# Splitting the loads of suf, pre and ekb into 2, 2 and 4 DMAs in a recurrent-attention and two-layer MoE kernel

## The chip, the cores and the metric

The kernel runs on one core of a Trainium2 chip. The metric is the device time of one execution in microseconds (us), median of the runs. Five engines work side by side, each through its own list of instructions in a fixed order: PE (matmuls; PEld loads its weights), DVE, ACT and POOL (elementwise work), and SP, which here issues every DMA. The core has 16 DMA engines that move the data.

## The reference

Four batches, 8 heads, 768 steps, head size 40. A state of 40 x 40 per head is decayed, corrected by one row and one column, and read out:

```python
for t in range(S):
    y[:, :, t] = einsum('bhd,bhde->bhe', rt, state)
    Sa = einsum('bhde,bhe->bhd', state, at)
    state = state * wt[:, :, None, :] - einsum('bhd,bhe->bhde', Sa, bt) \
            + einsum('bhd,bhe->bhde', vt, kt)
```

The result, as 3072 tokens of 320 numbers, goes through two layers `g(x @ w_in) @ w_out` with 2048 hidden units; g is a piecewise square in the first layer and `s * relu(h)**2 + b` in the second. The weights come as 64-bit numbers and are turned into 32-bit ones on the chip.

## The kernel before

**Attention** goes in 24 chunks of 32 steps; two chunks make a unit, so there are 12 units, u = 0 to 11. For each unit three arrays are loaded into 104 partitions: `suf` (429 KB, rows of 4224 bytes) and `pre` (416 KB, rows of 4096 bytes), from which DVE makes products of the decays by scans (L375, L384), and `ekb` (832 KB, rows of 8192 bytes), keys and b, which are multiplied by `suf` (L445, POOL from the second unit on). PE forms `ap` from `ekb` and `xa` (L466); its copy `am` is stored to `ascr` (L479) and loaded again as `la` (L555) and `aa` (L585). DVE inverts a triangular matrix in `ln` from `la` in 15 steps of two instructions (L566, L569), the "inverse"; it is stored to `lscr` (L571) and loaded as `lt` (L589), which `pl` (L598), `pq` and `up` on PE need. From there a chain runs chunk by chunk: `xp`, `up`, `sp` (state), `tp`, `gg`, `py` (the chunk's output) and `ptx`.

`suf`, `pre` and `ekb` have one buffer each. The buffer of `pre` is also that of `am`: the next unit's `pre` can be loaded only when both stores to `ascr` have landed. The next `ekb` can be loaded when the unit's `ap` matmuls and the copies to `tk` and `tb` are through.

**The MoE** takes blocks of 256 tokens (two chunks) in layer 1 (L954 into `h`, L985 into `acc`) and 512 tokens in layer 2 (L964, L1003). Layer 1 runs between the attention's steps; layer 2 follows it. Before the first block has its input, PE runs matmuls on weights whose result is not used (L1034, the "spare matmuls"); their number is fixed when the program is written out.

**The order** of the instructions on every engine is written out by a planner (`Order`) that runs when the program is built. Every piece of work is a thread that yields operations with an assumed duration; the planner gives each engine the ready thread that is due first. For a DMA it assumes 475 ns of SP for each issue and bytes / 360 ns of transfer, and at most eight DMAs on their way at a time. `dma(nbytes, fn, count, flag)` yields such an operation; `count` is the number of DMAs that `fn` issues. So a changed count changes the planned times, and with them the order on all five engines. On the chip the DMAs use eight completion semaphores in turn: each waits until the DMA eight before it has landed.

Of the kernel before, what the change touches and what calls it, by code (L numbers as in the profile page):

```python
# [221 lines left out]
def dma(nbytes, fn, count=1, flag=None, each=475):  # L222

    op = Op("SP", each * count, fn, 980, flag, nbytes / 360)
    op.count = count
    return op
# [22 lines left out]
def fast_path(ctx, tc, inside, ws_em, wp_em, a_em, kb_em, v_em, r_em, v_tok, eye, mask_a, mask_g, eye_kb,  # L249
              w1_in, w1_out, w2_in, w2_out, sb, out):  # L250
    nc = tc.nc
# [136 lines left out]
    tks, tes, lt_t = {}, {}, {}  # L388
    both = lambda n, c: ((n + "0", c), (n + "1", c))

    def loads_e():
        for u in range(NU):
            yield due("loads", u)
            yield Acq("es")
            suf = emp.tile([104, 2 * NP, C + 1], F32, tag="es", name="suf")
            yield dma(104 * 4224, lambda: nc.sync.dma_start(out=suf.rearrange("p a t -> p (a t)"), in_=ws_em[u]), 1, ("lw", u + 1))
            sufs[u] = suf

            def pre():
                yield Acq("ew")  # L400
                pre = emp.tile([104, 2 * NP, C], F32, tag="ew", name="pre")
                pres[u] = pre
                yield dma(104 * 4096, lambda: nc.sync.dma_start(out=pre.rearrange("p a t -> p (a t)"), in_=wp_em[u]), 1, ("lp", u + 1))

            def keys():
                yield Acq("ekb")
                ekb = emp.tile([104, 2, 2 * NP, C], F32, tag="ekb", name="ekb")
                ekbs[u] = ekb
                yield dma(104 * 8200, lambda: nc.sync.dma_start(out=ekb.rearrange("p x a t -> p (x a t)"), in_=kb_em[u]), 1, ("lk", u + 1))

            if u == 0:
                yield from pre()
            yield from keys()
            if u:
                yield from pre()
# [651 lines left out]
    for g in (loads_e(), loads_a(), setup(), clear(), prep_a(), inverse(), loads_x(), mend(), keys(), decays(), loads_t(), loads_v(), loads_r(),  # L1067
              chain_a(), chain_b(), warm(), ychunk(), xchunk(), moe(), loads_w(0), loads_w(1),
              *(convert(l, part, odd) for l in range(2) for part in range(2) for odd in range(2))):
        od.add(g, 0, Start.ready)  # L1070
# [94 lines left out]
def rwkv_moe_kernel(tc, out, **ins):  # L1165
    nc = tc.nc
    with tc.tile_pool(name="flag", bufs=1, space=DRAM) as fp:
        flag = fp.tile([1, 1], I32, name="flag")
        nat = {n: ins.pop(n) for n in "rkvwab"}
        with tc.manual_schedule():  # L1170
            fast_path(tc, flag, out=out, **ins)
        inside = nc.values_load(flag[0:1, 0:1], min_val=0, max_val=128)
        with tc.If(inside < 128):
            general_path(tc, nat, ins["eye"], ins["w1_in"], ins["w1_out"], ins["w2_in"], ins["w2_out"], ins["sb"], out)
# [66 lines left out]
```

## Time and profile before

| | |
|---|---|
| median of 3 runs | 1236.17 us (1234.88 to 1250.49) |
| the profiled execution: its time, its span | 1242.7 us, 1240.9 us |
| PE, PEld busy | 1125.5 us (91%), 1025.2 us (83%) |
| DVE, ACT, POOL busy | 736.5 us (59%), 757.4 us (61%), 360.9 us (29%) |
| moved by DMA | 107.36 MB |

The span is the time from the first to the last instruction in the trace. Busy shares are over the whole span; a start stage (to about 160 us), a stage with attention and layer 1 together (to about 700 us), the rest of layer 1 (to about 870 us) and layer 2 differ from one another. In a timeline, the bracket behind a row gives how long the engine stood idle before it and what ended that wait. In a chain of waits, a DMA's piece runs from its issue to its landing.

### The profile page before, as it was taken

To read this page: it belongs to the slowest core of one execution; us is meant where nothing else is said; L and a number is where in the kernel's file an instruction comes from. 1 tells how busy PE (TensorE), PEld (TensorE's weight loads), DVE (VectorE), ACT (ScalarE), POOL (GpSimd) and SP (SyncE) were. 2 spreads that over 40 slices of the span, in tenths; PEclk is the share of its full clock that TensorE was granted. 3 is DMA by queue.
4 is the path that set the end of the run, shared out by engine and by line. 5 is a ranking of instruction groups with operands and counts; after the bars stand their busy time and mean duration, and the time that the engine had idled before them with its cause. 6 is when DMAs were issued, how large, how long until landed. Compare 5 with 4: busy or idle time off the path is not lost.

```text
span 1240.9 us, 47386 instructions
## 1 busy us (share of the span) xinstructions
PE 1125.5 (91%) x20654; PEld 1025.2 (83%) x20654; DVE 736.5 (59%) x1629; ACT 757.4 (61%) x1537; POOL 360.9 (29%) x333
## 2 busy tenths in 40 slices
PE   3897899889898989989899999999999999999995
PEld 3796788778787778878788889999888889888895
DVE  4775877666568676777647343277974344444432
ACT  2433767557476565765666677688765555555553
POOL 5555563414143331323421112366540000000000
PEclk9898699899899988989999999999999999999998
DMA  7875525464555546474432210156201010101000
GB/s 195 239 199 138 125 58 124 91 140 99 110 108 109 124 95 126 81 149 104 96 79 61 44 43 14 34 172 205 69 1 48 1 47 4 45 10 26 16 7 24
DMA packets 188415, 107.36 MB, mean 87 GB/s; under 512 B 149126, under 2 KB 167686, under 8 KB 186950
## 3 DMA queue, kind: packets, MB, share of 16 engines
q1 hardware_dynamic: 188198, 104.24, 35.4%
q8 instruction: 164, 2.69, 0.9%
q14 instruction: 53, 0.43, 0.1%
HBM read 78.25 MB, written 19.66 MB: 79 GB/s over the span
## 4 chain that ended last, share of the span: by engine, by line
PE 72%; DVE 8%; ACT 5%; issue 5%; DMA 5%; SPq 1%; POOL 1%; DVEq 0%; ACTq 0%; POOLq 0%
PE h L954 14%; PE h L964 12%; PE acc L985 12%; PE acc L1003 12%; PE h L1034 6%; PE gg L819 2%; PE sp L747 2%; PE tq L768 2%; PE ap L466 2%; PE py L840 1%; PE xp L709 1%; PE up L724 1%; DMA lt<-lscr 1%; PE tp L802 1%; PE ptx L873 1%
## 5 line engine op out<-in xcount | busy, mean ns | idle before, releaser
L934 POOL TENSOR_TENSOR gl<-g,gh 128x512 fp32r<-128x512 f32 x96 | 125.4, 1306 | 433.9 <-ACT gh L932 380.0
L954 PE MATMUL h<-xh,w 128*128 128x256 f32 x1152 | 228.1, 301 | 5.7 <-DVE g L922 2.9
L954 PEld LDWEIGHTS h<-xh,w 128*128 128x128 f32 x1152 | 182.2, 198 | 12.4 <-issue 3.9
L985 PE MATMUL acc<-w,gh 128*128 128x320 f32 x768 | 190.6, 335 | 0.0
L1003 PE MATMUL acc<-w,gh 128*128 128x320 f32 x768 | 173.1, 312 | 2.6 <-ACT o L1016 2.1
L932 ACT CAST gh<-g 128x512 fp32r<-128x512 f32 x192 | 118.9, 619 | 61.1 <-DVE g L922 37.1
L1003 PEld LDWEIGHTS acc<-w,gh 128*128 128x128 f32 x768 | 132.2, 189 | 11.6 <-ACT o L1016 3.9
L934 DVE TENSOR_TENSOR gl<-g,gh 128x512 fp32r<-128x512 f32 x96 | 68.1, 709 | 117.7 <-ACT gh L932 117.5
L985 PEld LDWEIGHTS acc<-w,gh 128*128 128x128 f32 x768 | 130.9, 198 | 5.0 <-issue 0.2
L985 PE MATMUL acc<-w,gl 128*128 128x320 f32 x384 | 123.0, 320 | 0.0
L1003 PE MATMUL acc<-w,gl 128*128 128x320 f32 x384 | 118.7, 309 | 0.0
L928 ACT ACTIVATE g<-g,sbt 128x512 f32<-128x512 f32 x96 | 78.3, 816 | 64.8 <-DVE g L926 64.7
L954 PE MATMUL h<-xl,w 128*128 128x256 f32 x384 | 111.5, 290 | 0.4 <-issue 0.4
L922 DVE SCALAR_TENSOR_TENSOR g<-h,g 128x512 f32<-128x512 f32 x96 | 66.1, 688 | 75.1 <-ACT h L921 46.4
L919 ACT ACTIVATE g<-h,sbt 128x512 f32<-128x512 f32 x96 | 65.9, 687 | 64.8 <-PE h L954 61.7
L926 DVE SCALAR_TENSOR_TENSOR g<-h,g 128x512 f32<-128x512 f32 x96 | 66.3, 691 | 60.7 <-ACT g L925 60.6
L925 ACT ACTIVATE g<-h 128x512 f32<-128x512 f32 x96 | 57.2, 596 | 72.1 <-PE h L964 72.1
L1034 PE MATMUL h<-w 128*128 128x256 f32 x668 | 91.5, 299 | 0.0
L1034 PEld LDWEIGHTS h<-w 128*128 128x128 f32 x668 | 87.1, 204 | 1.4 <-issue 0.3
L238 POOL TENSOR_TENSOR t<-t,w 128x384 int32<-128x384 int32 x64 | 67.6, 1060 | 68.3 <-DVE t L236 41.0
L759 DVE TENSOR_TENSOR xr<-sp,pc 40x320 f32<-40x320 f32 x92 | 44.8, 487 | 58.4 <-PE sp L747 56.9
L964 PE MATMUL h<-xx,w 128*128 128x512 f32 x288 | 76.8, 402 | 2.1 <-DVE w L330 2.1
(107 smaller groups left out, 2277.7 us busy)
## 6 DMA issues: line engine op xcount, KB each, us to landing
w<-in_w_in SPq DMA_DIRECT2D x32, 384.0 KB
w<-in_w_out SPq DMA_DIRECT2D x32, 320.0 KB
ekb<-in_kb_em SPq DMA_DIRECT2D x12, 832.0 KB
tk<-ekb SPq DMA_DIRECT2D x48, 128.0 KB
suf<-in_ws_em SPq DMA_DIRECT2D x12, 429.0 KB
pre<-in_wp_em SPq DMA_DIRECT2D x12, 416.0 KB
xa<-in_a_em SPq DMA_DIRECT2D x48, 80.0 KB
xr<-in_v_tok SPq DMA_DIRECT2D x48, 80.0 KB
```

The lines of the kernel that those rows point to most:

```text
L238: (pool, n, lambda: nc.gpsimd.tensor_tensor(out=t, in0=t, in1=lo, op=ALU.add)),
L919: yield act(512, lambda: nc.scalar.activation(out=g, in_=h, func=AF.Relu, bias=sbt[:, 2:3]), more=93)
L922: yield dve(512, lambda: nc.vector.scalar_tensor_tensor(out=g, in0=h, scalar=1.0, in1=g, op0=ALU.subtract, op1=ALU.add))
L926: yield dve(512, lambda: nc.vector.scalar_tensor_tensor(out=g, in0=h, scalar=0.0, in1=g, op0=ALU.max, op1=ALU.mult))
L928: yield act(512, lambda: nc.scalar.activation(out=g, in_=g, func=AF.Identity, scale=sbt[:, 0:1], bias=sbt[:, 1:2]), more=230)
L932: yield act(512, lambda: nc.scalar.copy(out=gh, in_=g))
L934: yield mk(512, lambda: eng.tensor_tensor(out=gl, in0=g, in1=gh.bitcast(F32), op=ALU.subtract))
L954: yield pe(8 * 118, lambda: [nc.tensor.matmul(h[:, i, :], lhsT=a, rhs=b, start=m == 0, stop=m == 7) for m, (a, b) in enumerate(mm)])
L964: yield pe(4 * 224, lambda: [nc.tensor.matmul(h, lhsT=a, rhs=b, start=4 * i + m == 0, stop=4 * i + m == 7) for m, (a, b) in enumerate(mm[4 ...
L985: yield pe(6 * 147, lambda: [nc.tensor.matmul(acc[0, n][u], lhsT=a, rhs=b, start=p == 0 and m == 0, stop=p == NFF // 2 - 1 and m == 5) for ...
L1003: yield pe(3 * 147, lambda: [nc.tensor.matmul(acc[1, n][u], lhsT=a, rhs=b, start=f == 0 and m == 0, stop=f == NFF - 1 and m == 2) for m, ( ...
L1034: yield pe(2 * 109, lambda: [nc.tensor.matmul(h[:, i, :], lhsT=wh[:, 0:128], rhs=wh[:, 0:256], start=True, stop=True) for i in range(2)], ...
```

## The change

The three loads go through a new helper that cuts the rows of an array into k equal parts and issues one DMA for each. `suf` and `pre` become two DMAs of 104 rows of 2112 and 2048 bytes, `ekb` four of 104 rows of 2048 bytes. The planner is told the new counts. What is loaded, and where to, stays.

```diff
+    def pieces(out, src, k):
+        n = src.shape[-1] // k
+        for i in range(k):
+            nc.sync.dma_start(out=out[:, i * n:i * n + n], in_=src[:, i * n:i * n + n])
+
...
-            yield dma(104 * 4224, lambda: nc.sync.dma_start(out=suf.rearrange("p a t -> p (a t)"), in_=ws_em[u]), 1, ("lw", u + 1))
+            yield dma(104 * 4224, lambda: pieces(suf.rearrange("p a t -> p (a t)"), ws_em[u], 2), 2, ("lw", u + 1))
...
-                yield dma(104 * 4096, lambda: nc.sync.dma_start(out=pre.rearrange("p a t -> p (a t)"), in_=wp_em[u]), 1, ("lp", u + 1))
+                yield dma(104 * 4096, lambda: pieces(pre.rearrange("p a t -> p (a t)"), wp_em[u], 2), 2, ("lp", u + 1))
...
-                yield dma(104 * 8200, lambda: nc.sync.dma_start(out=ekb.rearrange("p x a t -> p (x a t)"), in_=kb_em[u]), 1, ("lk", u + 1))
+                yield dma(104 * 8200, lambda: pieces(ekb.rearrange("p x a t -> p (x a t)"), kb_em[u], 4), 4, ("lk", u + 1))
```

In all, 827 DMAs become 887, and 668 spare matmuls become 650; every other count of instructions stays. Lines behind the helper lie five further down in the changed kernel (L445 is L450 there). Three places show how the order moves.

**DVE at the start.** Before, the first rows after the scans of `suf` (t<-w is the first weight, turned to 32 bits):

```order
L384 SCALAR_TENSOR_TENSOR pre<-pre,start_p 104x256
L235 TENSOR_SCALAR t<-w 128x384
L383 RECIPROCAL start_p<-suf 104x8
L236 SCALAR_TENSOR_TENSOR t<-w,t 128x384
L384 SCALAR_TENSOR_TENSOR pre<-pre,start_p 104x256
L235 TENSOR_SCALAR t<-w 128x320
L445 TENSOR_TENSOR ekb<-ekb,suf 104x1024 x2
```

The same place in the changed kernel:

```order
L383 RECIPROCAL start_p<-suf 104x8
L384 SCALAR_TENSOR_TENSOR pre<-pre,start_p 104x256
L450 TENSOR_TENSOR ekb<-ekb,suf 104x1024 x2
L459 TENSOR_TENSOR xa_112<-xa_112,pre 40x512 x2
L459 TENSOR_TENSOR xa_113<-xa_113,pre 40x512 x2
L235 TENSOR_SCALAR t<-w 128x384
L236 SCALAR_TENSOR_TENSOR t<-w,t 128x384
```

The work on the weights, which stood among that on `pre`, `ekb` and `xa`, now stands behind all of it. On SP the first two weight loads move from behind `mska` to behind all eight `xa` loads.

**PE up to the first `pl`.** Before:

```order
L1034 MATMUL h<-w 128x256 x84
L466 MATMUL ap<-ekb,xa_113 32x64 x32
L1034 MATMUL h<-w 128x256 x30
L709 MATMUL xp<-xr_102,xa_112 32x40 x32
L1034 MATMUL h<-w 128x256 x212
L466 MATMUL ap<-ekb,xa_114 32x64 x32
L1034 MATMUL h<-w 128x256 x14
L466 MATMUL ap<-ekb,xa_115 32x64 x32
L1034 MATMUL h<-w 128x256 x198
L598 MATMUL pl<-lt,aa 32x16 x32
```

And now:

```order
L1039 MATMUL h<-w 128x256 x70
L471 MATMUL ap<-ekb,xa_113 32x64 x32
L1039 MATMUL h<-w 128x256 x48
L714 MATMUL xp<-xr_102,xa_112 32x40 x32
L1039 MATMUL h<-w 128x256 x216
L471 MATMUL ap<-ekb,xa_114 32x64 x32
L1039 MATMUL h<-w 128x256 x10
L471 MATMUL ap<-ekb,xa_115 32x64 x32
L1039 MATMUL h<-w 128x256 x182
L603 MATMUL pl<-lt,aa 32x16 x32
```

The spare matmuls ahead of the first `pl` go from 538 to 526, and those behind it from 130 to 124.

**SP around the `ekb` load of u = 4.** Before:

```order
L571 DMA lscr2_166<-ln_105 64x512 x2
L409 DMA ekb_3594<-in_kb_em 104x2048
L479 DMA ascr3_155<-am_3350 128x8x32
L694 DMA ggr_108<-in_r_em 40x512 x2
L589 DMA lt_3550<-lscr2_166 128x8x32
L403 DMA pre_3678<-in_wp_em 104x1024
L555 DMA la_3599<-ascr3_155 64x16x16 x2
```

And now:

```order
L394 DMA ekb_3561<-in_kb_em 104x512 x4
L699 DMA ggr_108<-in_r_em 40x512 x2
L484 DMA ascr3_155<-am_3328 128x8x32
L576 DMA lscr2_166<-ln_105 64x512 x2
L594 DMA lt_3659<-lscr2_166 128x8x32
L560 DMA la_3658<-ascr3_155 64x16x16 x2
L394 DMA pre_3706<-in_wp_em 104x512 x2
```

The store to `lscr` now stands behind `ekb`, and `la` stands ahead of `pre`. Such swaps go both ways over the units: a store to `lscr` stands close behind `ekb` in three units before (u = 3, 7, 11) and in three now (u = 3, 4, 6).

## Rows read from the trace of the kernel before

**Rows 1.** The page: share of the span by engine.

```profile
span 1240.9 us, 47386 instructions
PE 1125.5 (91%) x20654; PEld 1025.2 (83%) x20654; DVE 736.5 (59%) x1629; ACT 757.4 (61%) x1537; POOL 360.9 (29%) x333
```

**Rows 2.** Busy us by stage; PEclk is the granted clock's share, DMA the engines'.

```profile
core 0: us, PE busy (x) PEld busy (x) DVE busy (x) ACT busy (x) POOL busy (x), PEclk, DMA share, GB/s
0.00:160.00 160.00, 123.39 (x2257) 116.51 (x2258) 113.20 (x239) 68.16 (x161) 86.98 (x89) 0.87 0.68 177
160.00:700.00 540.00, 481.77 (x13925) 432.18 (x13924) 361.40 (x937) 342.11 (x753) 177.15 (x145) 0.92 0.48 102
700.00:870.00 170.00, 167.82 (x2529) 160.57 (x2529) 85.07 (x161) 132.35 (x261) 67.67 (x63) 1.00 0.29 91
870.00:1241.00 371.00, 352.53 (x1949) 315.92 (x1947) 176.85 (x294) 214.77 (x365) 29.07 (x36) 0.98 0.09 24
```

**Rows 3.** Chain that ended last: shares of the span by engine.

```profile
PE 72%; DVE 8%; ACT 5%; issue 5%; DMA 5%; SPq 1%; POOL 1%; DVEq 0%; ACTq 0%; POOLq 0%
```

**Rows 4.** The chain in order of time: start us, us, what.

```profile
214.70 6.70 DMA lt<-lscr
...
266.60 4.28 DMA lt<-lscr
...
324.34 2.38 DMA lscr<-ln
...
378.16 5.36 DMA ascr<-am
383.66 4.56 DMA pre<-in_wp_em
...
587.79 6.88 DMA lscr<-ln
594.72 2.42 DMA lt<-lscr
```

**Rows 5.** Timeline of SP around three `ekb` loads: start us, us, instruction.

```profile
78.14 0.40 SPq L409 DMA_DIRECT2D ekb<-in_kb_em  x1
78.65 0.38 SPq L479 DMA_DIRECT2D ascr<-am  x1
...
89.66 0.33 SPq L403 DMA_DIRECT2D pre<-in_wp_em  x1
...
212.50 0.50 SPq L409 DMA_DIRECT2D ekb<-in_kb_em  x1
...
586.28 0.31 SPq L409 DMA_DIRECT2D ekb<-in_kb_em  x1
```

**Rows 6.** Columns as Rows 2, stretches with one kind of load each.

```profile
5.10:7.20 2.10, 0.00 (x0) 0.00 (x0) 2.00 (x4) 1.28 (x1) 2.10 (x3) 1.00 1.05 250
7.20:11.80 4.60, 0.00 (x0) 0.00 (x0) 3.09 (x7) 0.25 (x1) 3.46 (x4) 1.00 0.85 191
12.50:15.50 3.00, 0.00 (x0) 0.00 (x0) 2.16 (x6) 2.29 (x5) 1.06 (x1) 1.00 0.70 251
329.70:335.10 5.40, 4.33 (x200) 3.84 (x201) 4.96 (x10) 2.93 (x8) 0.61 (x1) 1.00 0.84 178
337.50:340.20 2.70, 2.08 (x14) 1.99 (x14) 0.01 (x1) 1.62 (x4) 0.00 (x0) 0.59 0.93 191
```

**Rows 7.** What SP waited for in 0 to 13 us: total, times, longest.

```profile
SPq L424 <- DMA ekb<-in_kb_em: 4.3, 1, 4.3
SPq L424 <- DMA pre<-in_wp_em: 1.7, 1, 1.7
SPq L424 <- DMA suf<-in_ws_em: 0.9, 1, 0.9
```

**Rows 8.** DVE and PE at the end of the first inverse (timeline).

```profile
94.03 0.69 DVE L384 TENSOR_TENSOR_SCAN pre<-pre,start_p 104x256 f32<-104x256 f32 x1 [4.22 <-DMA w<-in_w_in]
...
105.58 1.05 PE L598 MATMUL pl<-lt,aa 32*32 32x16 f32 x64 [5.36 <-issue]
```

**Rows 9.** The page: the spare matmuls, busy and mean ns of one.

```profile
L1034 PE MATMUL h<-w 128*128 128x256 f32 x668 | 91.5, 299 | 0.0
```

**Rows 10.** DVE in the first 20 us (timeline).

```profile
13.34 0.36 DVE L235 TENSOR_SCALAR t<-w 128x384 int32<-128x384 int32 x1 [2.88 <-ACT w L233]
13.74 0.56 DVE L236 SCALAR_TENSOR_TENSOR t<-w,t 128x384 int32<-128x384 int32 x1
```

**Rows 11.** SP's issue of `pre` and `ekb`: ns min/median/max.

```profile
L403 SPq DMA_DIRECT2D pre<-in_wp_em x12: 307/316/2103, 1.3 to 595.5; - x12
L409 SPq DMA_DIRECT2D ekb<-in_kb_em x12: 308/367/662, 1.6 to 586.3; - x12
```

## The prediction

> **What bounds the kernel now.** I read the page first for the busy shares, then the busy time by stage, then the chain of waits, and last the timelines of SP and DVE around the three loads that change. The page [rows 1] says that PE is the engine to watch: 91% busy, no other over 61%. The stages [rows 2] say where the other 9% lie. From 700 to 870 us PE works 167.82 of 170 us, and layer 2 is nearly as full up to its last stores; none of the three loads is issued there, and nothing can be gained. In the start stage PE is idle for 160 - 123.39 = 37 us, and from 160 to 700 us for 540 - 481.77 = 58 us. Those 95 us are all that a change in loads can work on, and only the part that ends in a DMA: 5% of the chain, 62 us over the whole span, is DMA [rows 3].
>
> The pieces of the chain [rows 4] tell which DMAs. They are hardly the three loads: once it is `pre` (4.56 us), otherwise `lt`, `lscr` and `ascr`, small transfers of 128 KB or less that take 2.38 and 2.42 us when they go alone, and 6.70 and 6.88 us in two other places. SP's timeline [rows 5] has the reason: the 6.70 us at 214.70 start 2.2 us after an `ekb` load was issued (212.50), the 6.88 us at 587.79 1.5 us after another (586.28). A small transfer issued behind the 832 KB of `ekb` lands when those are through. So `ekb` costs by what waits behind it, about 4.4 us each time (6.88 - 2.38, 6.70 - 2.42).
>
> **The `ekb` load in four.** The bytes stay. What may change is their rate, and the trace has no load of 104 rows of 2 KB, so it is bounded. From 7.20 to 11.80 us nearly all that moves is `ekb`, rows of 8 KB: 191 GB/s with the DMA engines 85% busy, so they are at work and slow [rows 6]. From 12.50 to 15.50 us, mostly `xa` loads with rows of 2 KB and weight rows of 3 KB, 251 GB/s come out of only 70%. One end: no gain. Other end: `ekb`'s 13 of 16 engines (104 rows in equal shares) at the second stretch's rate per busy engine, 251 / 0.70 x 13/16 = 291 GB/s, or 852 kB in 2.9 us instead of 4.5 us at 191 GB/s: 1.5 us less. The nearest row is `pre`, half the row length on the same 104 partitions: in the middle of the run it moved at 191 GB/s against 178 for `ekb` [rows 6], 7% better for a row half as long, which would be 0.3 us. The rows halve twice, and the early stretch of `pre` (250 GB/s, partly `ekb`'s own bytes) speaks for more. I take 0.7 us per load, estimated between these rows, ends 0 and 1.5 us. The rate pays where something on the chain stands behind `ekb`: four places in rows 4 (214.70, 266.60, 378.16 with 383.66, 587.79), and one at the start. There `ekb` is issued at 78.14, the store to `ascr` behind it at 78.65, `pre`, which needs that store, only at 89.66 [rows 5]; DVE stands 4.22 us in the middle of the inverse until 94.03 for its scan of `pre`, 4.4 us after that issue, although the wait is labelled with a weight [rows 8]. Five places by 0.7 us: **-3.5 us**; ends 0 and 11 loads by 1.5, -16.5 us.
>
> Three more issues at 0.37 us (median, [rows 11]) put the next DMA on SP 1.1 us later. What hides that is `ekb` itself: what stands behind waits over 4 us for its bytes, not for its issue. Taken at 0; if that cover went, five places by 1.1, +5.5 us.
>
> On batching, the Trainium skill (DMA: Bandwidth & Descriptors, Rules for kernel authors) says the opposite of this change: for most bandwidth, 128 partitions and at least 1 MiB per DMA, and many small transfers should be coalesced into one. By that alone 832 KB in one DMA would be better than in four of 208 KB, and the sum would turn positive. The trace does not agree in the stretch just named: DMAs of at most 384 KB moved 251 GB/s there, against 191 for one of 832 KB.
>
> **`suf` and `pre` in two.** One more issue each, 0.32 us for `pre` [rows 11], against a somewhat better rate. `suf` is loaded long before its scans; only `pre` is on the chain. I put the two at 0, ends 0.3 us either way at five places, 1.5 us.
>
> **The new order at the start.** 18 spare matmuls fewer, at 91.5 / 668 = 0.137 us [rows 9], are 2.5 us. Twelve of them stand ahead of the first `pl`, where PE idles 5.36 us anyway [rows 8]: they shorten nothing. The six behind it: **-0.8 us**. The `pl` wait itself ends with the first inverse on DVE. Up to there DVE has one first and two second steps of a weight fewer (0.36 + 2 x 0.56 us, [rows 10]) and one scan of `pre` fewer (0.69, [rows 8]): 2.2 us. And DVE no longer idles 2.88 us for the first weight between two scans of the first `pre` [rows 10], since the weights now stand behind. On the other side the first two weight loads go behind all `xa` loads. DMAs go at most eight at a time: the ninth to eleventh waited for `suf`, `pre` and `ekb`, 0.9, 1.7 and 4.3 us [rows 7]. The eight pieces now fill that allowance alone, so the first weights land some 2 to 3 us later (by the length of the `xa` stretch, 12.50 to 15.50), and the spare matmuls with them. I take **-2 us** of the 5.36; ends -5.36 and +3 us.
>
> **The sum.** -3.5 - 0.8 - 2 = -6.3 us against the profiled execution of 1242.7 us (span 1240.9): 1236.4 us. That execution lies 6.5 us above the median 1236.17 us of the runs; against the median the forecast is **1230 us**. The ends: -16.5 - 1.5 - 0.8 - 5.4 gives 1212, +5.5 + 1.5 + 3 gives 1246.
>
> **Rivals.** *The row length is not what slows `ekb`.* The slow rate may belong to 104 partitions on 13 engines; `pre` and `ekb` are within 7% in mid-run (191, 178). Then only the start's -2.8 us are left: 1233 us. Chance 0.20. The Trainium skill (SBUF — State Buffer, Door 1: The DMA port swizzle) has DMA bandwidth depend on how many of SBUF's ports the partitions reach; by it pieces on the same partitions would gain nothing. The rates of rows 6 do not exclude that.
>
> *The full gain*: 291 GB/s, and all 11 later loads count, with the start's best: about 1212 us. For it: engines busy and slow in every `ekb` stretch. Against it: in seven units nothing of `ekb` is on the chain. Chance 0.10.
>
> *The new order is the worse one.* In u = 4 the store to `lscr` now stands behind `ekb`: 6.88 instead of 2.38 us, +4.5. There `lt` stood behind `ekb` before (6.70 instead of 2.42 us), which gives most back; in u = 6 `lt` stood ahead, and the 4.5 us are lost. Two or three such places: 1230 + 14 = 1244 us. Against it: as many stores stand behind `ekb` before as now. Chance 0.17.
>
> *Slower: the eight DMAs at a time become the bound.* Four of the eight are now pieces of one `ekb`. If the awaited `lt` or `la` is beyond the eighth, it is issued only when pieces have landed, and its own 2.4 us [rows 4] come after `ekb` instead of beside it: 11 x 2.4 = 26 us, 1262 us. It decides when over four DMAs stand between `ekb` and the awaited one; in u = 4 there are five ahead of `lt`. Against it: the pieces land one by one, so the first slot comes free early. Chance 0.05.
>
> *Slower: every piece pays its own start and landing.* `lt` alone takes 2.42 us [rows 4] for 131 kB, 0.5 us of them at 251 GB/s: 1.9 us fixed. If three pieces more per `ekb` and one per `pre` paid that one after another, four by 1.9 at five places are 38 us: 1274 us with nothing won on the rate. Against it: the 251 GB/s of small loads in flight together. Chance 0.03.
>
> The forecast (1222 to 1238 us) has the other 0.45. About 2%, 24.7 us, is what a measurement of this kernel can tell from no change: faster means below 1211, slower above 1261. Half of the full gain reaches below 1211: faster 0.06. The two slower rivals make 0.07 with a little for the worse order. Within 2%: 0.87. The range for 8 in 10 leaves out the lower half of the full gain and the slower rivals, and takes in the worse order up to the upper end of the sum: 1213 to 1246 us. The likeliest case's own range is 1222 to 1238.
>
> **What would show it.** Right: in the stretch of an `ekb` load more GB/s than 178 to 191; small transfers behind it that land in less than 6.7 us; less than 4.22 us of DVE waiting inside the first inverse, and a first `pl` before 105.58 us. Wrong: the same GB/s with four pieces; waits of SP for a landed piece ahead of `lt` or `la`; a PE idle time from 160 to 700 us above 58 us, which would mean that the order, not the loads, decides.

## The result, and the profile after

The changed kernel takes 1222.8 us (median of 20 runs, 1216.55 to 1229.6) against 1239.18 us of the kernel before on the same chip (20 runs, 1229.04 to 1250.49): a ratio of 0.986, 95% interval [0.984, 0.9879], or 17 us. The forecast of 1230 us was on the right side of no change and 7 us too slow; its sum had 6.3 us of gain. Executions of one kernel scatter by 1 to 2.5%, so every ratio below stands with its 95% interval; one whose interval takes in 1 is no change that can be told.

The page of the changed kernel, with the shares by engine as in [rows 1]:

```profile
span 1219.8 us, 47452 instructions
PE 1110.5 (91%) x20636; PEld 1007.8 (83%) x20636; DVE 742.0 (61%) x1629; ACT 755.0 (62%) x1537; POOL 363.1 (30%) x333
```

PE's idle time over the span fell from 1240.9 - 1125.5 = 115.4 us to 109.3 us, only 6 us. PE's busy time fell by 15.0 us, although only 18 matmuls went. The stages after, columns as in [rows 2]:

```profile
0.00:160.00 160.00, 124.30 (x2276) 117.38 (x2277) 113.69 (x248) 67.56 (x158) 86.44 (x91) 0.91 0.65 179
160.00:700.00 540.00, 490.87 (x14584) 437.60 (x14584) 379.88 (x959) 359.85 (x798) 183.18 (x147) 0.96 0.46 103
700.00:870.00 170.00, 167.56 (x1971) 159.19 (x1970) 94.07 (x175) 133.44 (x262) 77.41 (x77) 1.00 0.30 95
```

From 160 to 700 us PE idles 49 us instead of 58, and the granted clock is 0.96 instead of 0.92; at the start 0.91 instead of 0.87. In the same 540 us PE does 14584 instead of 13925 matmuls. So the time came from two things that go together here: shorter waits, and more of the work at the higher of the two clock levels. The place where both are easiest to see is the end of the first inverse. Columns as before, here of the kernel before:

```profile
100.00:105.00 5.00, 0.23 (x2) 0.02 (x1) 3.62 (x5) 0.00 (x0) 3.37 (x4) 0.75 0.92 235
105.00:110.00 5.00, 3.65 (x135) 3.28 (x136) 1.48 (x4) 0.78 (x3) 4.18 (x4) 0.50 0.72 124
```

and of the changed kernel:

```profile
100.00:105.00 5.00, 3.52 (x181) 3.25 (x184) 3.93 (x5) 1.29 (x5) 4.85 (x4) 1.00 0.81 181
105.00:110.00 5.00, 4.56 (x187) 4.17 (x174) 1.59 (x4) 2.19 (x5) 3.35 (x4) 1.00 0.90 243
```

Before, PE stood still for nearly all of 100 to 105 us, and from 105 to 110 us it ran at 0.50, the 1.2 GHz level. After, it worked on, and the clock stayed at 1.00. A little later (115 to 120 us) the changed kernel has its own stretch at 0.50, so the dip is not always avoided.

The rows that answer to [rows 8], from the timeline of DVE and PE after:

```profile
90.94 0.69 DVE L384 TENSOR_TENSOR_SCAN pre<-pre,start_p 104x256 f32<-104x256 f32 x1 [0.26 <-DMA pre<-in_wp_em]
...
100.92 0.72 PE L603 MATMUL pl<-lt,aa 32*32 32x16 f32 x64 [1.80 <-issue]
```

The wait of 4.22 us inside the first inverse is 0.26 us, and the first `pl` starts at 100.92 instead of 105.58 us.

The DMAs that others wait for, up to 700 us (total us, times, longest). The kernel before:

```profile
DVE tmp L566 <- DMA la<-ascr: 13.0, 7, 3.4
DVE pre L384 <- DMA pre<-in_wp_em: 4.5, 2, 3.8
DVE pre L384 <- DMA w<-in_w_in: 4.2, 1, 4.2
PE pl L598 <- DMA lt<-lscr: 10.4, 6, 3.4
POOL ln L560 <- DMA lscr<-ln: 6.1, 4, 2.1
```

The changed kernel:

```profile
DVE tmp L571 <- DMA la<-ascr: 9.4, 6, 3.0
DVE pre L384 <- DMA pre<-in_wp_em: 1.5, 2, 1.3
PE pl L603 <- DMA lt<-lscr: 7.6, 5, 4.0
POOL ln L565 <- DMA lscr<-ln: 1.2, 1, 1.2
```

Ahead of the scans of `pre` 7.2 us of DVE waiting went, ahead of `pl` and the small transfers 11.3 us. (The longest group, `en` on `lt`, grew from 18.6 to 21.1 us.) The chain of waits of the changed kernel cannot be set against [rows 3] and [rows 4]: its pieces end in layer 2, where PE alone fills it.

Where the gain stands in the program, by the group of `py`, a product that every one of the twelve units needs (ns min/median/max, first and last start). Before:

```profile
L840 PE MATMUL py<-kbs,ggr x1536: 196/200/277, 124.3 to 775.3; 128*32 128x40 f32 x96, 104*32 104x40 f32 x96
```

After:

```profile
L845 PE MATMUL py<-kbs,ggr x1536: 196/200/276, 119.5 to 749.3; 128*32 128x40 f32 x99, 104*32 104x40 f32 x93
```

The first `py` is 4.8 us earlier, the last 26.0 us; at the end of the span 21.1 us are left. Of the 4.9 us lost behind it, 3.1 us have a name: in layer 2 PE waits 5.2 us for weights from DVE (`h` on `w`, 2 times), where it waited 2.1 us before.

The rate of `ekb`, which the forecast rested on: stretches between an issue and the landing of its last piece, columns as in [rows 6]. Before:

```profile
376.50:382.20 5.70, 5.11 (x103) 4.50 (x95) 5.34 (x19) 4.71 (x12) 1.27 (x1) 1.00 0.82 188
431.00:437.30 6.30, 5.00 (x149) 4.37 (x142) 4.97 (x12) 3.08 (x5) 1.66 (x3) 1.00 0.91 179
587.20:592.80 5.60, 5.60 (x45) 5.59 (x44) 3.94 (x10) 3.27 (x5) 0.79 (x1) 1.00 0.87 208
```

After:

```profile
368.70:374.60 5.90, 5.37 (x212) 4.78 (x211) 5.35 (x13) 3.85 (x12) 1.65 (x3) 1.00 0.83 202
415.90:421.50 5.60, 5.33 (x122) 4.66 (x121) 5.35 (x13) 4.16 (x8) 1.67 (x3) 1.00 0.83 206
577.20:582.30 5.10, 5.10 (x153) 4.69 (x152) 1.99 (x5) 3.80 (x10) 1.27 (x1) 1.00 0.83 211
```

In the first two of each, at about the same busy share of the DMA engines (0.82 and 0.91 before, 0.83 after), 202 and 206 GB/s instead of 188 and 179. In the third it is 211 instead of 208. Three more loads, read in the same way, went from 191, 178 and 252 GB/s to 224, 190 and 259. So the rate rose at all six, by 1 to 17%, with the DMA engines busier by 0.01 at the most; other transfers move in these stretches as well, so the rates are not those of `ekb` alone.

### The profile page after: what moved, and what is told of

The parts are those of the page before. It is cut to its first block, busy times and chain, and to the rows that moved or that the text cites. A ratio compares the mean times of both kernels' runs of the same rounds, so it can differ in the third digit from the quotient of the medians.

```text
span 1219.8 us, 47452 instructions
## 1 busy us (share of the span) xinstructions
PE 1110.5 (91%) x20636; PEld 1007.8 (83%) x20636; DVE 742.0 (61%) x1629; ACT 755.0 (62%) x1537; POOL 363.1 (30%) x333
## 5 line engine op out<-in xcount | busy, mean ns | idle before, releaser
L959 PE MATMUL h<-xh,w 128*128 128x256 f32 x1152 | 224.8, 298 | 1.9 <-DVE g L927 1.1
L959 PEld LDWEIGHTS h<-xh,w 128*128 128x128 f32 x1152 | 179.3, 194 | 8.6 <-DVE g L927 1.6
L1008 PEld LDWEIGHTS acc<-w,gh 128*128 128x128 f32 x768 | 132.4, 190 | 10.3 <-ACT o L1021 2.4
L990 PEld LDWEIGHTS acc<-w,gh 128*128 128x128 f32 x768 | 126.0, 192 | 5.0
L1039 PE MATMUL h<-w 128*128 128x256 f32 x650 | 89.1, 299 | 5.6 <-ACT w L329 4.7
L959 PEld LDWEIGHTS h<-xl,w 128*128 128x128 f32 x384 | 74.9, 195 | 3.3 <-DVE xl L884 3.3
```

Source lines behind the costliest of these rows:

```text
L959: yield pe(8 * 118, lambda: [nc.tensor.matmul(h[:, i, :], lhsT=a, rhs=b, start=m == 0, stop=m == 7) for m, (a, b) in enumerate(mm)])
L990: yield pe(6 * 147, lambda: [nc.tensor.matmul(acc[0, n][u], lhsT=a, rhs=b, start=p == 0 and m == 0, stop=p == NFF // 2 - 1 and m == 5) for ...
L1008: yield pe(3 * 147, lambda: [nc.tensor.matmul(acc[1, n][u], lhsT=a, rhs=b, start=f == 0 and m == 0, stop=f == NFF - 1 and m == 2) for m, ( ...
L1039: yield pe(2 * 109, lambda: [nc.tensor.matmul(h[:, i, :], lhsT=wh[:, 0:128], rhs=wh[:, 0:256], start=True, stop=True) for i in range(2)], ...
```

## The experiments

The theory after the result: **loads**, the pieces themselves pay, with rival **order**, the changed order of the program (which follows from telling the planner of 2, 2 and 4 DMAs) pays. In all experiments but one the planner is told of one DMA per load, so the order is that of the kernel before and only the DMAs differ. Diffs are against the kernel before (the helper `pieces` is added as in the change); lines not shown are as before.

**All three in pieces, order of before.**

```diff
+            yield dma(104 * 4224, lambda: pieces(suf.rearrange("p a t -> p (a t)"), ws_em[u], 2), 1, ("lw", u + 1))
...
+                yield dma(104 * 4096, lambda: pieces(pre.rearrange("p a t -> p (a t)"), wp_em[u], 2), 1, ("lp", u + 1))
...
+                yield dma(104 * 8200, lambda: pieces(ekb.rearrange("p x a t -> p (x a t)"), kb_em[u], 4), 1, ("lk", u + 1))
```

> The DMAs are split as in the change, but the planner is told one DMA for each load, so all engines keep the order of the kernel before. Theory 'loads' (the split itself pays: faster rate, or scans that start when the first piece has landed): ratio to before 0.984 to 0.989, as for the change, the wait of DVE for pre inside the first inverse falls from 4.22 us to under 1.5 us. Theory 'order' (the new plan pays, the split is only its occasion): 0.998 to 1.004, that wait stays near 4 us. The prediction's own sum has 3.5 us for the rate of ekb in this kernel: 0.997.

Measured 0.9884 [0.983, 0.9938]. **Single DMAs in the new order** (the same three lines with 1 piece each, and 2, 2 and 4 told to the planner):

```diff
+                yield dma(104 * 8200, lambda: pieces(ekb.rearrange("p x a t -> p (x a t)"), kb_em[u], 1), 4, ("lk", u + 1))
```

> The planner is told 2, 2 and 4 DMAs, so all engines have the order of the change, but each load is one DMA as before. Theory 'order': ratio to before 0.984 to 0.990, granted clock near 0.965, first pl near 101 us. Theory 'loads': 0.998 to 1.004 or slower, since the order then counts on something that does not come; first pl near 105 us. The prediction's own sum has 2.8 us for the order: 0.998.

Measured 1.0034 [0.9987, 1.0081]. So the order by itself gives nothing, and most of the gain, perhaps all (the intervals overlap), is there without it: *loads* holds, *order* falls. Two rows of this kernel, the groups of `pl` and of `py`, say a little more (ns min/median/max, first and last start):

```profile
L603 PE MATMUL pl<-lt,aa x1536: 171/178/231, 100.6 to 708.2; 32*32 32x16 f32 x192
...
L845 PE MATMUL py<-kbs,ggr x1536: 196/200/276, 121.4 to 775.8; 128*32 128x40 f32 x97, 104*32 104x40 f32 x95
```

The first `pl` starts 5 us earlier than before (100.6 against 105.58), as the theory *order* had it, but that brought no time: the last `py` starts at 775.8 us, half a microsecond later than in the kernel before. What the start gave was lost on the way. (This profiled execution took 1246.56 us, 9 us over the median of its kernel, so how much was lost, and where, is not to be read from it.)

**`ekb` alone in four, order of before.**

```diff
-                yield dma(104 * 8200, lambda: nc.sync.dma_start(out=ekb.rearrange("p x a t -> p (x a t)"), in_=kb_em[u]), 1, ("lk", u + 1))
+                yield dma(104 * 8200, lambda: pieces(ekb.rearrange("p x a t -> p (x a t)"), kb_em[u], 4), 1, ("lk", u + 1))
```

> Only ekb is split in four, in the order of the kernel before. If the rate of ekb with rows of 2 KB is what pays, most of what all three splits give in the old order shows here: ratio within 0.002 of that kernel's, and small transfers behind ekb land in under 6 us instead of 6.7 to 6.9. If the rate does not rise (178 to 191 GB/s as before), 0.999 to 1.003.

Measured 0.993 [0.9895, 0.9964]: a gain, but not within 0.002 of the 0.9884, so `ekb` pays for a part and neither of the two ranges was met.

**`pre` alone in two, order of before.**

```diff
-                yield dma(104 * 4096, lambda: nc.sync.dma_start(out=pre.rearrange("p a t -> p (a t)"), in_=wp_em[u]), 1, ("lp", u + 1))
+                yield dma(104 * 4096, lambda: pieces(pre.rearrange("p a t -> p (a t)"), wp_em[u], 2), 1, ("lp", u + 1))
```

> Only pre is split in two, in the order of the kernel before. If the gain comes from scans that start on the first piece of pre: 0.992 to 0.996 and the wait of DVE for pre inside the first inverse is about 1 us shorter than 4.22 us. If it comes from ekb or from the order: 0.999 to 1.002.

Measured 0.9938 [0.9901, 0.9976], about as much as `ekb`, where the forecast had 0. The scans of `pre` go in four groups of 8 of its 32 slices, and the first two need only the first half. So a theory for `pre`: **early half**, DVE starts on the half that has landed. Its test is the same traffic with the second half first.

**`pre` in two, second half first.**

```diff
-        for i in range(k):
+        for i in reversed(range(k)):
```

> As the kernel that splits only pre in two in the old order (ratio 0.9938), but the second half is issued first, so the half that DVE scans first lands last; bytes, rows and number of DMAs are the same. Theory 'early half' (the gain is that the first two of four scans wait for the first half alone): no gain left, 0.998 to 1.004. Theory 'rate' (two DMAs with shorter rows land sooner as a whole): still 0.992 to 0.996.

Measured 1.0033 [0.9994, 1.0073], as *early half* has it, but the test is weak. The split in two was measured beside a kernel before of 1238.4 us, this one beside one of 1233.52 us on another chip; their own medians, 1231.25 and 1234.33 us, are only 3.1 us apart. **`pre` in four**, measured beside the reversed one, should gain at least as much:

```diff
+                yield dma(104 * 4096, lambda: pieces(pre.rearrange("p a t -> p (a t)"), wp_em[u], 4), 1, ("lp", u + 1))
```

> Only pre is split, in four instead of two, in the old order: each of the four scans has its own DMA. Theory 'early half': the first quarter lands at most about 0.6 us before the first half did, in six units at most 4 us: 0.990 to 0.995. Theory 'each piece costs' (start, landing, eight DMAs at a time): 0.997 or more. If two pieces are all that pays, as for the split in two, 0.994.

Measured 1.0026 [0.9985, 1.0067] (1233.67 us): a miss. The idle time of DVE ahead of the scans of `pre` (us, times) in the kernel with two pieces:

```profile
  DMA pre<-in_wp_em: 1.7, 2
```

with the second half first:

```profile
  DMA pre<-in_wp_em: 4.9, 3
```

and in four:

```profile
  DMA pre<-in_wp_em: 0.7, 1
```

The wait moves as *early half* says: 8.7 us before (4.5 + 4.2), 1.7 in two, 4.9 reversed, 0.7 in four. But with the least wait the time did not fall. DVE's wait for `pre` is thus not what sets the time by itself, and the 0.9938 stands without a cause that the runs support; it may be the comparison.

**`suf` alone in two** (`pieces(suf..., ws_em[u], 2), 1` in its line, as in the first experiment):

> Only suf is split in two, in the old order. suf is loaded long before its scans, so all theories have 0.998 to 1.002; the product of the runs with ekb alone and pre alone, 0.993 x 0.9938 = 0.987, against 0.988 for all three, leaves nothing for it.

Measured 1.0024 [0.9981, 1.0066]: nothing, as forecast.

**`ekb` in one DMA, issued from ACT's queue.** If small transfers wait behind `ekb` only because they stand in the same queue, another queue would free them.

```diff
-                yield dma(104 * 8200, lambda: nc.sync.dma_start(out=ekb.rearrange("p x a t -> p (x a t)"), in_=kb_em[u]), 1, ("lk", u + 1))
+                yield dma(104 * 8200, lambda: nc.scalar.dma_start(out=ekb.rearrange("p x a t -> p (x a t)"), in_=kb_em[u]), 1, ("lk", u + 1))
```

> Nothing is split; ekb is issued from ACT's DMA queue instead of SP's, at the same place in the plan. If what ekb costs is that the small transfers behind it in the same queue wait for its bytes: those land in 3 to 5 us instead of 6.7 to 6.9, and the ratio is 0.98 to 0.99. If the DMA engines themselves are the limit, with either queue: the small transfers keep landing at 6 us or more, 0.997 to 1.003. If ACT's waits for the free buffer cost more than the queue gains: over 1.005.

Measured 1.022 [1.016, 1.028]. The trace shows a new wait, SP's own, from 60 to 720 us (total, times, longest):

```profile
SPq L694 <- DMA ekb<-in_kb_em: 34.2, 5, 12.8
SPq L479 <- DMA ekb<-in_kb_em: 16.4, 2, 11.5
...
SPq L543 <- DMA ekb<-in_kb_em: 8.6, 1, 8.6
SPq L245 <- DMA ekb<-in_kb_em: 7.4, 1, 7.4
```

In the kernel before SP waits for `ekb` in that stretch not once. With the load on another engine's queue, SP stood 66.6 us for its landing, and everything behind stood with it. So this run says what such a move costs here, and not cleanly what a small transfer does behind `ekb`. One place says something of it: SP's timeline of this kernel,

```profile
147.78 0.39 SPq L479 DMA_DIRECT2D ascr<-am  x1
149.19 5.42 SPq L694 DMA_DIRECT2D ggr<-in_r_em  x2
154.93 0.31 SPq L403 DMA_DIRECT2D pre<-in_wp_em  x1
```

where `pre` needs the store to `ascr`. After its 4.7 us for `ekb` (inside the 5.42), SP waited 0.2 us more for `ascr`, which had been issued 7.15 us earlier, just behind `ekb` (147.62 us, ACT's queue). A store that takes some 2.4 us alone (`lscr`, of the same size, [rows 4]) took 7 us with nothing of `ekb` ahead of it in its own queue.

**What of `ekb` pays?** Three theories: *row length* (shorter rows move faster), *any cut* (others get in between any four DMAs), *early piece* (the consumer starts on the first quarter). Three cuts tell them apart, all in the order of before. `ekb` in four, last quarter first (the loop of `pieces` reversed, for `ekb` alone):

> ekb alone in four DMAs of 2 KB rows, last quarter issued first, order of before. Theories 'row length' and 'any cut': 0.993, since the traffic is the same. Theory 'early piece': 1.000, since POOL's first slices come last, as it was with pre reversed (1.0033).

Measured 0.9932 [0.9899, 0.9964]. `ekb` in four by partitions, rows of 8 KB:

```diff
+    def row_pieces(out, src, k):
+        n = src.shape[0] // k
+        for i in range(k):
+            nc.sync.dma_start(out=out[i * n:i * n + n], in_=src[i * n:i * n + n])
...
+                yield dma(104 * 8200, lambda: row_pieces(ekb.rearrange("p x a t -> p (x a t)"), kb_em[u], 4), 1, ("lk", u + 1))
```

> ekb alone in four DMAs cut by partitions (26 each), so the rows stay 8 KB, order of before. Theory 'row length': 1.000, since no row is shorter. Theory 'any cut': 0.993, as with four DMAs of 2 KB rows. Theory 'early piece': 1.000, since every slice of ekb needs all four pieces. If a DMA on 26 partitions reaches fewer engines at a time, slower, 1.005 or more.

Measured 1.0052 [1.001, 1.0095]. `ekb` in two, rows of 4 KB (`pieces(ekb..., kb_em[u], 2), 1`):

> ekb alone in two DMAs, rows of 4 KB, order of before. Theory 'row length' (the rate and the wait behind ekb follow the row): about half of the 0.7%, 0.996. Theory 'early piece' (POOL starts on what has landed): most of it, 0.995. Theory 'any cut' (transfers behind get in between pieces): 0.996. A value of 1.000 or more would say that two pieces are not enough. This run tells little between them alone; it is read with the next two.

Measured 0.9963 [0.9926, 1.0001]. *Early piece* falls with the first (reversed, and the gain is the same). *Any cut* has the second against it, and the third lies in the middle, though its interval takes in 1: *row length* is the theory that is left. The second is not clean, since 1.0052 is also what the last branch of its expectation had, that 26 partitions reach fewer DMA engines at a time. The packets speak against that branch. The page's line on the main DMA queue says it without a clock or a chain (packets, MB, share of 16 engines' span). Before:

```profile
q1 hardware_dynamic: 188198, 104.24, 35.4%
```

`ekb` in four:

```profile
q1 hardware_dynamic: 192410, 104.24, 34.6%
```

`ekb` in four by partitions:

```profile
q1 hardware_dynamic: 188666, 104.24, 35.3%
```

Twelve loads of 104 rows in four pieces each are 3744 rows more by columns (104 x 3 x 12) and none more by partitions. What is left of the packets is 468 more in both, 13 for each of the 36 added DMAs. By this estimate a piece of 26 partitions was spread over as many engines as one of 104.

Share times span is the time that one of the 16 engines worked, on the mean, for all DMAs of this queue. The rounding of the share is 0.6 us, but kernels with the same DMAs differ by up to 2.8 us (439.3 and 441.9, 434.8 and 432.0):

| kernel | row of the load | DMA time, us | ratio |
|---|---|---|---|
| before | `ekb` 8 KB, `pre`, `suf` 4 KB | 0.354 x 1240.9 = 439.3 | 1 |
| `ekb` by partitions | 8 KB | 436.9 | 1.0052 |
| `ekb` in two | 4 KB | 431.4 | 0.9963 |
| `ekb` in four | 2 KB | 427.6 | 0.993 |
| `ekb` in four, reversed | 2 KB | 427.8 | 0.9932 |
| `pre` in two; reversed | 2 KB | 434.8; 432.0 | 0.9938; 1.0033 |
| `pre` in four | 1 KB | 429.2 | 1.0026 |
| `suf` in two | 2 KB | 432.9 | 1.0024 |
| `ekb` in four and `pre` in two | 2 KB | 422.6 | 0.9944 |
| single loads, new order | 8 KB, 4 KB | 441.9 | 1.0034 |
| all three, order of before | 2 KB | 418.5 | 0.9884 |
| the change | 2 KB | 418.4 | 0.986 |

The same bytes on the same partitions take 11.7 us less in four pieces by columns, and 2.4 us less, no more than the scatter, in four by partitions. For `pre` and `suf` the DMA time falls as well, by 4 to 10 us, but no gain in time that repeats came with it. Nor is the row the whole law: from 4 to 2 KB `ekb` saved 3.8 us, and `pre`, of half the bytes, 4.5 and 7.3 us. What waits behind `ekb` is seen on SP, which holds a DMA back until the one it needs has landed (60 to 720 us; total, times, longest). Before:

```profile
SPq L403 <- DMA ascr<-am: 19.4, 5, 6.9
...
SPq L589 <- DMA lscr<-ln: 15.1, 9, 5.7
```

`ekb` in four:

```profile
SPq L394 <- DMA ascr<-am: 18.6, 5, 5.3
...
SPq L594 <- DMA lscr<-ln: 11.6, 8, 4.5
```

`ekb` in four, reversed:

```profile
SPq L394 <- DMA ascr<-am: 16.0, 5, 4.9
...
SPq L599 <- DMA lscr<-ln: 12.1, 8, 4.8
```

In the same order of instructions the longest waits for a small transfer are 0.9 to 2.0 us shorter, and both sums fall. The longest wait on `ascr` bears the comparison with the other kernels in the order of before: 4.9 to 5.7 us in all four that have `ekb` in four by columns, 5.5 with `ekb` in two, 7.6 by partitions, and 6.7 to 7.1 in all five that load it from SP in one DMA. The sum does not: it goes from 18.9 to 24.6 us among those five.

**`ekb` in four with `pre` in two, `suf` whole, order of before** (the two lines shown for each alone): does what is left add up?

> ekb in four and pre in two, suf whole, order of before. If the two gains add and suf adds nothing: 0.993 x 0.9938 = 0.987, as the whole change (0.986). If ekb and pre remove the same waits, so that one gain covers the other: 0.993. If the whole change needed suf's halves too: 0.990 or more.

Measured 0.9944 [0.9902, 0.9987], beside 0.9932 for reversed `ekb` alone in the same comparison: `pre` added nothing to `ekb`, or `suf`'s halves were needed too, which is the last branch of the expectation. This is no better version than the change, and its interval leaves out the whole change's 0.986.

## Why the prediction was right, and where its sizes were off

**What bounds.** Right: the gain came ahead of 700 to 775 us, and nothing was won above. But the argument counted PE's idle time alone. Between the two profiled executions (21.1 us) 6 us are idle time, 2.4 us the 18 spare matmuls (91.5 - 89.1 us), and 12.6 us are the other matmuls taking less time, at a mean clock of 0.965 instead of 0.943. This part had no term. It is no fixed companion of a saved wait: `ekb` alone had 10 us less idle time (105.5 us) at 0.942, reversed it had 102.8 us at 0.956. What makes the clock follow in one execution and not in another is open.

The clocks of all executions say how much hangs on it. The 93 executions of the kernel before that stand beside the experiments had mean granted clocks of 0.931 to 0.957, 0.946 on the mean; the 20 of the change had 0.950 to 0.965, 0.956 on the mean. Seven of the 93 had 0.955 to 0.957, and took 1218.9 to 1225.5 us; the seven of the change at these clocks took 1220.9 to 1226.6 us. At the same clock the two kernels took the same time, so nearly all of the gain goes with the change being at a low clock less often. `ekb` in four is alike in part: 0.949 and 0.952 on the mean beside 0.945 and 0.947 of the kernel before. Whether the shorter waits keep the clock up, as at the end of the first inverse, or something else does, no run here separates.

**The `ekb` load in four, -3.5 us.** The mechanism was right as far as the runs show it, a load that moves faster, with shorter waits behind it. The size was not. "0.7 us per load" was near: the DMA engines worked 11.7 / 12 = 0.97 us less per load, on the mean of the 16. The term that was mis-sized is "five places by 0.7 us", which counts places of one chain: `ekb` in four alone gave 0.7% in two comparisons on two chips, 0.007 x 1238.4 = 8.7 us. That is 0.7 us at each of the 12 loads, but the agreement does not show that every load counts: by the clocks above, a part of the 8.7 us may be the higher clock that the sum had no term for. One of the five places was also misread: the `lt` at 266.60 was issued ahead of its `ekb` (268.46 on SP's timeline), not behind it. And the place at the start does not settle the size: from the issue of `ekb` to that of `pre` it took 11.5 us before, 10.4 and 10.0 in four and 12.3 by partitions, but 10.6 also with `ekb` whole and `pre` in two. "Three more issues ... taken at 0" stands: the gain is net of them.

The rival that row length is not the cause has the cut by partitions against it, and that pieces on the same partitions gain nothing is refuted by the 0.7% and the 11.7 us. The batching rule of the Trainium skill (DMA: Bandwidth & Descriptors, Rules for kernel authors) asks for DMAs of at least 1 MiB for most bandwidth. The runs do not go its way here: 832 KB in one DMA was slower than in four of 208 KB by 0.7%, and had more DMA time for the same bytes.

**"I put the two at 0"** (`suf` and `pre`). For `suf` alone that was right. For `pre` the runs disagree: 0.9938 alone in two pieces, but 1.0033 reversed and 1.0026 in four, both beside the kernel before on another chip, and nothing on top of `ekb`. Not settled.

**The new order, -0.8 and -2 us.** The place was right, 5 us at the first `pl` (100.6 us with single DMAs); the sum wrong, since it had no term for giving that back later. The first weight is read 4.6 us later in the change (17.36 instead of 12.76 us, "2 to 3" was forecast), but the spare matmuls did not move with it: they start at 21.06 instead of 21.43 us. The rival "the new order is the worse one" named one way to lose it, a store to `lscr` behind `ekb`; that this was the way was not tried.

**The slower rivals.** Neither came. From 60 to 720 us SP never waits for a piece of `ekb` in the changed kernel, and no piece paid a fixed cost that shows: more pieces, less DMA time.

**What stays open.** `ekb` in four, alone, gives 8 to 9 of the 17 us. The other 8 come when `suf`, `pre` and the order are changed with it, though none of the three does it reliably alone. All three loads in the order of before (0.9884) are closer to the change than `ekb` and `pre` are (0.9944), but those two intervals overlap, and so neither `suf` in company nor the order in company is shown.

## What to carry to other kernels

Where small transfers that the end waits for stand behind a large load, look at the length of the load's rows as well as at its place: the queue's packet time for the same bytes shows what shorter rows save, and a cut that leaves the rows long tells it from a mere split. DMA time saved need not be time saved; `pre` and `suf` saved as much per byte and gave nothing that repeats. Count the places from all the waits of the kind, not from the one chain that happened to end last, and do not trust a wait that vanished until the time has moved with it. Set the times of two kernels against their granted clocks before a gain is shared out among waits, and compare two variants only where both were measured on one chip beside the same runs of the kernel before.

## What the runs showed of the hardware

- On 104 partitions, 2 KB rows cost the DMA engines less than 8 KB rows for the same bytes: with 12 loads of 832 KB cut so, the queue's time per engine over the whole kernel fell from 439.3 to 427.6 us, with 4 KB in between (431.4), and to 436.9 only where the four pieces kept rows of 8 KB. For `pre` 1 KB rows (429.2) were cheaper than 4 KB ones (439.3).
- A 128 KB store issued 0.16 us behind `ekb` from another queue took some 7 us to land, so at that one place another queue did not free it.
- Moving one load to ACT's queue cost 1.022 [1.016, 1.028], with 66.6 us of waits of SP for that load.
